# A batch's output products in one run over four PSUM banks, as 64-row and 64 by 64 tiles, and gamma's loads moved behind the first queries

## The chip, the cores and the metric

The kernel runs on one core of one Trainium2 chip. The metric is device microseconds of one execution. All ratios below are the mean time of one kernel's fast runs over the mean of the other's fast runs of the same rounds, so they are not quite the ratio of the medians that are quoted beside them. Under 1 is faster than the kernel before. The 95% interval is given in brackets.

The engines are TensorE (PE: matmuls; PEld: its weight loads), VectorE (DVE), ScalarE (ACT), GpSimd (POOL) and SyncE (SP, which issues most DMAs). L346 is a line of the kernel's source; the line numbers of the changed kernel differ from those of the kernel before.

## The reference, cut to what matters

A linear attention without softmax, a per-head norm, and then a gated feed-forward layer on all 4608 tokens:

```python
batch, n_heads, seq, head_dim = (8, 8, 576, 64)
kv  = np.einsum('bhsd,bhse->bhde', k, v)          # a 64 x 64 state per head
out = np.einsum('bhsd,bhde->bhse', q, kv)         # "output products"
out = out / sqrt(mean(out**2, axis=-1) + 1e-6) * g_norm
x   = out as [batch*seq, 512]
xn  = x / sqrt(mean(x**2, axis=-1) + 1e-6) * rms_g
y   = silu(xn @ w_gate) * (xn @ w_val) @ w_out    # d_ff = 1536
```

## The kernel before

Each batch has 576 tokens: 512 "main" tokens, and 64 "tail" tokens. The tails of all eight batches form a ninth block of 512. The feed-forward layer of block n runs in 16 units: units 0 to 11 are the up products (two groups of four 128x512 matmuls each, into `g_ps` and `v_ps`), units 12 to 15 the down products. Between those units the kernel places the attention of block n+1: state products, output products, squares, sums, norm.

The output products of a main block multiply transposed queries `qt` (two heads of 64 on 128 rows, 512 tokens) with a block-diagonal state `kv_all` (two 64x64 states on the diagonal of 128x128, zeros elsewhere). One group of 128 tokens took four 128x128 matmuls, at four different units:

```python
def o_products(self, c, ps):
    for j in range(NS):                      # NS = 4 pairs of heads
        cols = ps[:, 2 * j : 2 * j + 2, :]   # 128 columns of one PSUM bank
        if self.tail:
            for u in range(2):               # two batches' 64 tail tokens
                rows = slice(u * TAIL, (u + 1) * TAIL)
                PE.matmul(cols[rows], lhsT=tails_q["t"][:, c, j, rows],
                          rhs=kv_all[:, 2 * c + u, j, :], ...)
        else:
            PE.matmul(cols, lhsT=self.qt[:, j, 128 * c : 128 * c + 128],
                      rhs=kv_all[:, self.n, j, :], ...)
...
kv0, os = (3, (4, 5, 6, 7)) if n == 1 else (1, (2, 3, 5, 6))
steps[kv0] += [a.kv_products, a.kv_copy]     # a = attention of block n+1
for c, u in enumerate(os):
    cs = ((0, 1), (), (2, 3), ())[c] if a.tail else (c,)
    steps[u].append(lambda a=a, cs=cs: a.o_rows(cs))   # products
    steps[u].append(lambda a=a, c=c: a.put_o(c))       # squares and copy on ScalarE
    steps[u + 1].append(lambda a=a, c=c: a.sums(c))    # sums on VectorE
```

The opening handles batch 0 by hand. Its loads are issued in this order on the sync queue (the values of 0 and 1 on ScalarE's); index j is a pair of heads:

```python
for j in (0, 1):
    load_kv(0, "k", nc.sync, ...j);  load_kv(0, "v", nc.scalar, ...j)
load_q0(0, nc.sync)                                  # "the first queries"
for j in (2, 3):
    load_kv(0, "k", nc.sync, ...j);  load_kv(0, "v", nc.sync, ...j)
nc.sync.dma_start(out=gam[0:NS, :], in_=moe_rms_g...)     # gamma, 2 KB
nc.sync.dma_start(out=gam[NS:NS+1, :]..., in_=g_norm...)  # gamma, 0.5 KB
load_q0(1, nc.sync)
...                                                  # then the weights
```

For n = 1, ScalarE casts the values of batch 2 in units 0 and 1:

```python
steps[0] += [lambda i=i: cast_kv(2, "v", i, SC) for i in (0, 1)]
steps[1] += [lambda i=i: cast_kv(2, "v", i, SC) for i in (2, 3)]
```

## Time and profile before

| | before |
|---|---|
| median, range | 322.36 us (322.31 to 323.43, 3 runs) |
| span of the profiled run | 321.4 us |
| PE busy | 97% |
| granted PE clock | full on the page. But the page counts the stretch before the first clock record (5.2 us in this trace) as full, and there the 128x512 matmuls start 0.43 us apart, twice the later 0.216 us. In one trace the clock falls to half in the opening, from 13.0 to 16.4 us (see e4) |

The first lines are from the page of the kernel before: engine busy times, then rows of 40 slices of 8 us each, in tenths.

```profile
PE 311.0 (97%) x2011; PEld 154.1 (48%) x2047; DVE 179.6 (56%) x371; ACT 178.8 (56%) x319; POOL 20.3 (6%) x43
...
PE   7799999999999999999999999999999999999995
...
DMA  7999999987279747923893378948002600240014
...
PE 84%; DMA 10%; issue 1%; ACT 1%; another core or an unknown queue 1%; DVE 1%; SPq 0%; ACTq 0%
...
L346 PE MATMUL att_ps<-kv_all,qt 128*128 128x128 bf16 x96 | 9.3, 219 | 0.3
```

The reader sees two regimes: DMA is at 9 tenths or more in slices 2 to 8 (8 to 64 us), PE in all but the first two and the last. PE is the bound from about 62 us on (busy 63.62 of the 64 us from 62 to 126 us, 131.16 of the 132 us from 126 to 258 us). The L346 line lists the 96 main output products at 219 ns each, but within a group their records start 56 ns apart and overlap. What a run costs is therefore read from starts. These lines are the timeline of PE in the kernel before (start us, duration us, engine, line, operation, out<-in, count, and in brackets what idle time before it waited for), around one group of four output products, then around the two tail runs.

```profile
127.88 0.81 PE L479 MATMUL v_ps<-xnt,wv_sb 128*128 128x512 bf16 x3
128.53 0.39 PE L346 MATMUL att_ps<-kv_all,qt 128*128 128x128 bf16 x4
128.75 1.03 PE L479 MATMUL g_ps<-xnt,wg_sb 128*128 128x512 bf16 x4
...
258.35 0.81 PE L479 MATMUL v_ps<-xnt,wv_sb 128*128 128x512 bf16 x3
259.09 0.64 PE L341 MATMUL att_ps<-kv_all,qt 128*64 128x128 bf16 x16
259.66 0.60 PE L479 MATMUL g_ps<-xnt,wg_sb 128*128 128x512 bf16 x2
```

A 128x512 matmul starts every 0.216 us, so three from 127.88 us end their turn at 128.53 us. The four products then take until 128.75 us: 0.22 us, or 56 ns each. Four groups make 0.89 us a batch. In the tail, the turn ends at 259.00 us and the next 128x512 starts at 259.66 us: 0.66 us for 16 matmuls in 64-column tiles, 1.33 us for both tail runs. The first tail matmul comes 0.09 us late; here the tile in the records changes from `128*128` to `128*64`, and e6 below measures what a change of tiling costs.

The last two places are in the opening of the kernel before: the wait for gamma, and the wait at 61 us.

```profile
9.59 0.67 ACT L106 CAST vb<-st 128x576 bf16<-128x576 f32 x1 [0.97 <-DMA st<-in_v_dram]
10.32 0.47 PE L267 MATMUL att_ps<-vb,kb 64*64 64x64 bf16 x18 [0.55 <-ACT vb L106]
11.62 0.19 PE L715 MATMUL o_ps<-ident,gam 5*128 5x5 f32 x1 [0.84 <-DMA gam<-in_g_norm_dram]
12.39 0.47 PE L267 MATMUL att_ps<-vb,kb 64*64 64x64 bf16 x18
...
60.33 1.14 ACT L106 CAST vb<-st 128x512 bf16<-128x512 f32 x2 [2.15 <-DMA st<-in_v_dram]
62.01 0.38 PE L479 MATMUL g_ps<-xnt,wg_sb 128*128 128x512 bf16 x1 [0.26 <-ACT silu L484]
```

PE stands 0.84 us for gamma at 11.62 us. At 62.01 us it waits for a silu, which stood in ScalarE's queue behind casts that waited for the values of batch 2.

### The profile page before, as it was taken

The page shows a single profiled execution, that of the slowest core. Times are in us where ns is not written, and L with a number is a line of the kernel's source. Part 1 is how long each engine was busy: PE and PEld are TensorE (multiplying, and loading weights), DVE is VectorE, ACT ScalarE, POOL GpSimd, SP SyncE. Part 2 cuts the span into 40 slices and gives each one's busy share as a digit, 9 for nine tenths or more (in the row PEclk, how much of TensorE's full clock was granted, in tenths as well). Part 3 has the DMA queues.
Part 4 walks back from the last instruction along what each step waited for, and adds up shares of the span by engine and source line. Part 5 has one row for each costly group of instructions (what it writes and reads, how often), then busy time and mean ns, then how long its engine had stood idle before and what let it go on. Part 6 is the DMA issues. An engine that isn't in the chain of part 4 may idle for free.

```text
span 321.4 us, 5351 instructions
## 1 busy us (share of the span) xinstructions
PE 311.0 (97%) x2011; PEld 154.1 (48%) x2047; DVE 179.6 (56%) x371; ACT 178.8 (56%) x319; POOL 20.3 (6%) x43
## 2 busy tenths in 40 slices
PE   7799999999999999999999999999999999999995
PEld 3475456454445444544444444444544444444443
DVE  4685857569427932794279516951696058703310
ACT  3596457665767476647664766566554355233321
POOL 1253452100000000000000000000000000000000
PEclk9999999999999999999999999999999999999999
DMA  7999999987279747923893378948002600240014
GB/s 260 344 353 387 379 375 296 231 244 212 56 151 311 174 124 185 309 69 90 174 321 105 65 202 194 311 102 174 35 2 49 174 40 1 42 157 1 0 34 98
DMA packets 74439, 54.89 MB, mean 171 GB/s; under 512 B 42281, under 2 KB 67117, under 8 KB 74413
## 3 DMA queue, kind: packets, MB, share of 16 engines
q1 hardware_dynamic: 74044, 53.89, 59.9%
q10 hardware_dynamic: 368, 0.66, 0.6%
q8 instruction: 16, 0.26, 0.3%
q14 instruction: 11, 0.08, 0.1%
HBM read 37.75 MB, written 9.44 MB: 147 GB/s over the span
## 4 chain that ended last, share of the span: by engine, by line
PE 84%; DMA 10%; issue 1%; ACT 1%; another core or an unknown queue 1%; DVE 1%; SPq 0%; ACTq 0%
PE g_ps L479 27%; PE v_ps L479 26%; PE o_ps L521 24%; DMA st<-in_v_dram 3%; DMA st<-in_moe_w_out_dram 3%; PE att_ps L346 2%; DMA gam<-in_g_norm_dram 2%; DMA st<-in_k_dram 1%; PE att_ps L275 1%; DMA out_dram<-o_sb 1%; PE g_ps L496 1%; PE o_ps L496 1%; PE v_ps L496 1%; DVE xna L460 0%
## 5 line engine op out<-in xcount | busy, mean ns | idle before, releaser
L485 DVE TENSOR_TENSOR h_sb<-silu,v_ps 128x512 bf16<-128x512 bf16 x104 | 70.8, 683 | 107.8 <-ACT silu L484 68.7
L479 PE MATMUL g_ps<-xnt,wg_sb 128*128 128x512 bf16 x403 | 105.7, 379 | 1.3 <-ACT silu L484 0.3
L479 PE MATMUL v_ps<-xnt,wv_sb 128*128 128x512 bf16 x405 | 104.4, 379 | 0.1
L484 ACT ACTIVATE silu<-g_ps 128x512 bf16<-128x512 f32 x104 | 62.4, 601 | 61.9 <-PE g_ps L479 49.2
L521 PE MATMUL o_ps<-wo_sb,h_sb 128*128 128x512 bf16 x386 | 87.1, 379 | 0.5
L479 PEld LDWEIGHTS <-wv_sb 128*128 128x128 bf16 x416 | 40.7, 98 | 49.1 <-DVE wv_sb L204 0.2
L521 PEld LDWEIGHTS <-h_sb 128*128 128x128 bf16 x420 | 40.7, 98 | 47.9 <-issue 0.3
L479 PEld LDWEIGHTS <-wg_sb 128*128 128x128 bf16 x416 | 38.9, 98 | 42.3 <-issue 0.8
L106 ACT COPY o_sb<-o_ps 128x512 f32<-128x512 f32 (+1 forms) x34 | 19.7, 579 | 38.0 <-PE o_ps L521 35.3
L368 DVE TENSOR_REDUCE ssq<-sq 128x16 f32<-128x1024 bf16 x28 | 34.2, 1220 | 1.0
L359 ACT ACTIVATE sq<-att_ps 128x512 bf16<-128x512 f32 x28 | 16.7, 597 | 12.3 <-PE att_ps L346 7.9
L106 ACT CAST vb<-st 128x512 bf16<-128x512 f32 (+2 forms) x34 | 19.5, 626 | 5.7 <-DMA st<-in_v_dram 5.7
L385 DVE TENSOR_TENSOR xna<-outa,s1y 128x512 bf16<-128x512 bf16 x28 | 17.9, 684 | 0.0
L106 ACT CAST qb<-st 128x1024 bf16<-128x1024 f32 (+1 forms) x17 | 15.4, 943 | 2.3 <-DMA st<-in_q_dram 2.2
L361 ACT CAST outa<-att_ps 128x512 bf16<-128x512 f32 x28 | 16.3, 581 | 0.0
L106 ACT CAST kb<-st 128x512 bf16<-128x512 f32 (+1 forms) x25 | 14.0, 619 | 0.0
L367 DVE TENSOR_TENSOR sq<-sq,gsq 128x512 bf16<-128x512 bf16 x28 | 11.7, 418 | 0.0
L346 PEld LDWEIGHTS <-qt 128*128 128x128 bf16 x96 | 7.4, 98 | 5.7
L346 PE MATMUL att_ps<-kv_all,qt 128*128 128x128 bf16 x96 | 9.3, 219 | 0.3
L622 PE MATMUL att_ps<-kv_all 128*128 128x512 bf16 (+1 forms) x21 | 7.5, 486 | 1.2 <-DVE sel L611 1.2
L108 POOL CAST wo_sb<-st 128x512 bf16<-128x512 f32 x12 | 7.5, 654 | 7.0 <-DMA st<-in_moe_w_out_dram 7.0
L108 DVE CAST kb<-st 128x576 bf16<-128x576 f32 (+1 forms) x12 | 5.3, 459 | 2.5 <-DMA st<-in_k_dram 2.5
(139 smaller groups left out, 160.6 us busy)
## 6 DMA issues: line engine op xcount, KB each, us to landing
out_dram<-o_sb SPq DMA_DIRECT2D x14, 512.0 KB, 3.0
st<-in_q_dram SPq DMA_DIRECT2D x6, 1024.0 KB, 6.4
st<-in_k_dram SPq DMA_DIRECT2D x6, 1024.0 KB, 10.2
st<-in_v_dram SPq DMA_DIRECT2D x6, 1024.0 KB, 11.8
st<-in_moe_w_out_dram SPq DMA_DIRECT2D x6, 512.0 KB, 10.3
st<-in_moe_w_gate_dram SPq DMA_DIRECT2D x4, 512.0 KB, 8.4
st<-in_moe_w_val_dram SPq DMA_DIRECT2D x4, 512.0 KB, 9.1
st<-in_k_dram SPq DMA_DIRECT2D x4, 288.0 KB, 5.7
```

The lines of the kernel that those rows point to most:

```text
L106: engine.copy(out=dst, in_=src)
L108: engine.tensor_copy(out=dst, in_=src)
L346: PE.matmul(cols, lhsT=self.qt[:, j, 128 * c : 128 * c + 128], rhs=kv_all[:, self.n, j, :], start=(j == 0), stop=(j == NS - 1),)
L359: SC.activation(out=self.sq[c][:, 0], in_=ps, func=ACT.Square)
L361: SC.copy(out=self.outa[c], in_=ps)
L367: DVE.tensor_tensor(out=sq[:, 1], in0=sq[:, 0], in1=gsq8, op=OP.mult)
L368: DVE.reduce_sum(out=self.ssq[:, c], in_=sq, axis=AX.X)
L385: DVE.tensor_tensor(out=self.xna[c], in0=self.outa[c], in1=self.alpha[:, c, :].to_broadcast([128, H, D]), op=OP.mult)
L479: PE.matmul(ps, lhsT=wt[:, s, j * 128 : (j + 1) * 128], rhs=x[:, s, :], start=(s == 0), stop=(s == NS - 1),)
L484: SC.activation(out=silu, in_=g_ps, func=ACT.Silu)
L485: DVE.tensor_tensor(out=self.h[:, j, :], in0=silu, in1=v_ps, op=OP.mult)
L521: PE.matmul(self.o_ps[c], lhsT=self.h[:, j, c * 128 : (c + 1) * 128], rhs=wo_sb[:, j, :], start=(j == 0), stop=(j == NF - 1),)
```

## The change

The intent: use only the 64 rows and 64 columns that are not zero, let the two heads of a pair work in the two row halves of the array, do a whole block in one run (two banks of the attention pool and the two that the down products leave free), and fetch gamma before it is needed.

```diff
+        def o_products(self):
+            self.banks = [
+                [p.tile([128, 2, NS, D], FP32, name=nm) for _ in range(2)]
+                for p, nm in ((att_pool, "att_ps"), (ops_pool, "o_ps"))
+            ]
+            for c in range(T):
+                for j in range(NS):
+                    for g in range(2):                       # head parity = row half
+                        rows = slice(g * D, g * D + D)
+                        ps = self.banks[c // 2][g][:, c % 2, j, :]
+                        flags = ...
+                        if self.tail:
+                            for u in range(2):
+                                us = slice(u * TAIL, (u + 1) * TAIL)
+                                PE.matmul(ps[us], lhsT=tails_q["t"][rows, c, j, us],
+                                          rhs=kv_all[rows, 2 * c + u, j, rows], **flags)
+                        else:
+                            PE.matmul(ps, lhsT=self.qt[rows, j, 128 * c : 128 * c + 128],
+                                      rhs=kv_all[rows, self.n, j, rows], **flags)
...  # put_squares and put_rows read two banks each; pools regrouped in pairs
-            kv0, os = (3, (4, 5, 6, 7)) if n == 1 else (1, (2, 3, 5, 6))
+            kv0 = 1 + 2 * int(n == 1)
...
+            steps[kv0 + 1] += [a.o_products]
+            for i in range(2):
+                u = kv0 + 1 + 2 * i
+                steps[u] += [lambda a=a, i=i: a.put_squares(i)]
+                steps[u + 1] += [lambda a=a, i=i: a.put_rows(i)]
+                for c in range(2):
+                    steps[u + i + c] += [lambda a=a, c=2 * i + c: a.sums(c)]
...  # opening: gamma's two loads before keys and values 2, 3
     load_q0(0, nc.sync)
+    nc.sync.dma_start(out=gam[0:NS, :], ...)
+    nc.sync.dma_start(out=gam[NS : NS + 1, :]..., ...)
     for j in (2, 3):
         load_kv(0, "k", nc.sync, slice(j, j + 1))
         load_kv(0, "v", nc.sync, slice(j, j + 1))
-    nc.sync.dma_start(out=gam[0:NS, :], ...)
-    nc.sync.dma_start(out=gam[NS : NS + 1, :]..., ...)
...  # opening: weight rounding around the norm of the second half of batch 0
-    round_w(1, "g", 0, SC)
-    round_w(1, "g", 3, SC)
-    round_w(1, "g", 1, GP)
+    for s in range(2):
+        round_w(1, "g", s, GP)
     Z.head()
     Z.root_by_table(lambda: round_w(1, "g", 2, DVE))
+    round_w(1, "g", 3, SC)
```

More of the change, by code (lines that the diff above doesn't have):

```diff
@@ L59 @@
     qt_pool = pool("qt", 2)
-    outa_pool = pool("outa", 4)
-    sq_pool = pool("sq", 2)
+    outa_pool = pool("outa", 2)
+    sq_pool = pool("sq", 1)
     sqt_pool = pool("sqt", 1)
@@ L300, in __init__ @@
             self.sq = {}
-            self.o_ps = {}
             self.qt = None
@@ L333, in q_turn @@
             cast(engine, self.qt[:, :, 256 * pair : 256 * pair + 256], ps.rearrange("p j i t -> p j (i t)"))
-        def o_products(self, c, ps):
-            for j in range(NS):
-                cols = ps[:, 2 * j : 2 * j + 2, :]
-                if self.tail:
-                    for u in range(2):
-                        rows = slice(u * TAIL, (u + 1) * TAIL)
-                        PE.matmul(
-                            cols[rows], lhsT=tails_q["t"][:, c, j, rows], rhs=kv_all[:, 2 * c + u, j, :],
-                            start=(j == 0), stop=(j == NS - 1),
-                        )
-                else:
-                    PE.matmul(
-                        cols, lhsT=self.qt[:, j, 128 * c : 128 * c + 128], rhs=kv_all[:, self.n, j, :],
-                        start=(j == 0), stop=(j == NS - 1),
-                    )
@@ L351, in o_rows @@
-        def o_rows(self, cs):
-            for c in cs:
-                self.o_ps[c] = att_pool.tile([128, H, D], FP32, name="att_ps")
-                self.o_products(c, self.o_ps[c])
-        def put_o(self, c):
-            ps = self.o_ps[c]
-            self.sq[c] = sq_pool.tile([128, 2, H, D], BF16, name="sq")
-            SC.activation(out=self.sq[c][:, 0], in_=ps, func=ACT.Square)
-            self.outa[c] = outa_pool.tile([128, H, D], BF16, name="outa")
-            SC.copy(out=self.outa[c], in_=ps)
+        def o_products(self):
[8 more added lines that the diff above has]
+                        ps = self.banks[c // 2][g][:, c % 2, j, :]
+                        flags = dict(start=(c % 2 == 0 and j == 0), stop=(c % 2 == 1 and j == NS - 1))
+                        if self.tail:
+                            for u in range(2):
+                                us = slice(u * TAIL, (u + 1) * TAIL)
+                                PE.matmul(
+                                    ps[us], lhsT=tails_q["t"][rows, c, j, us], rhs=kv_all[rows, 2 * c + u, j, rows],
+                                    **flags,
+                                )
+                        else:
+                            PE.matmul(
+                                ps, lhsT=self.qt[rows, j, 128 * c : 128 * c + 128], rhs=kv_all[rows, self.n, j, rows],
+                                **flags,
+                            )
@@ new lines, in put_squares, with put_rows @@
+        def put_squares(self, i):
+            p, nm = ((sq_pool, "sq"), (sqt_pool, "sqt"))[i]
+            self.sq[i] = p.tile([128, 2, 2, H, D], BF16, name=nm)
+            for g in range(2):
+                SC.activation(out=self.sq[i][:, :, 0, g:H:2, :], in_=self.banks[i][g], func=ACT.Square)
+        def put_rows(self, i):
+            rows = outa_pool.tile([128, 2, H, D], BF16, name="outa")
+            for g in range(2):
+                SC.copy(out=rows[:, :, g:H:2, :], in_=self.banks[i][g])
+            for c in range(2):
+                self.outa[2 * i + c] = rows[:, c]
@@ L365, in sums @@
                 self.ssq = stat_pool.tile([128, T, 2, H], FP32, name="ssq")
-            sq = self.sq[c]
+            sq = self.sq[c // 2][:, c % 2]
             DVE.tensor_tensor(out=sq[:, 1], in0=sq[:, 0], in1=gsq8, op=OP.mult)
@@ L440, in o @@
             self.o_products(c, ps)
-            self.outa[c] = outa_pool.tile([128, H, D], BF16, name="outa")
+            if c % 2 == 0:
+                self.rows = outa_pool.tile([128, 2, H, D], BF16, name="outa")
+            self.outa[c] = self.rows[:, c % 2]
             cast(engine, self.outa[c], ps)
@@ L593 @@
     load_q0(0, nc.sync)
-    for j in (2, 3):
-        load_kv(0, "k", nc.sync, slice(j, j + 1))
-        load_kv(0, "v", nc.sync, slice(j, j + 1))
     nc.sync.dma_start(out=gam[0:NS, :], in_=moe_rms_g.rearrange("(s p) -> s p", p=128))
@@ L601 @@
     )
+    for j in (2, 3):
+        load_kv(0, "k", nc.sync, slice(j, j + 1))
+        load_kv(0, "v", nc.sync, slice(j, j + 1))
     load_q0(1, nc.sync)
@@ L985 @@
             a = atts[n + 1]
-            kv0, os = (3, (4, 5, 6, 7)) if n == 1 else (1, (2, 3, 5, 6))
+            kv0 = 1 + 2 * int(n == 1)
             if not a.tail:
                 steps[kv0] += [a.kv_products, a.kv_copy]
-            for c, u in enumerate(os):
-                cs = ((0, 1), (), (2, 3), ())[c] if a.tail else (c,)
-                steps[u].append(lambda a=a, cs=cs: a.o_rows(cs))
-                steps[u].append(lambda a=a, c=c: a.put_o(c))
-                steps[u + 1].append(lambda a=a, c=c: a.sums(c))
+            steps[kv0 + 1] += [a.o_products]
[3 more added lines that the diff above has]
+                steps[u + 1] += [lambda a=a, i=i: a.put_rows(i)]
+                for c in range(2):
+                    steps[u + i + c] += [lambda a=a, c=2 * i + c: a.sums(c)]
             late = 2 * int(n == 1)
```

## The prediction

> **What bounds the kernel now.** The page gives TensorE (PE) 311.0 of 321.4 us busy (97%), clock full in every slice; the chain of waits that ended last is 84% PE and 10% DMA. There are two regimes. Until about 62 us the DMA engines are 99-100% busy in the slices; the chain runs through a weight DMA and then the values of batch 2, landing at 60.3 us, and near 61.4 us PE idles 0.3-0.4 us behind it (ScalarE is held by casts of those values). From 62 to 314 us the timeline shows PE matmuls without a gap, one 128x512 every 216 ns. There only TensorE time counts: time saved on VectorE or ScalarE is worth nothing, unless it starts a stall.
>
> **What changes, costed.**
>
> 1. Output products of six batches (after 62 us). Before: four runs of four 128x128 matmuls, 55.7 ns from start to start, 16 x 55.7 = 0.89 us per batch, no change of tiling. After: one run of 32 matmuls with 64 rows, 64 columns moving, even and odd heads in alternating row halves. If two halves overlap, a pair should cost what pairs of 64-wide column tiles cost in the state products: 31.6 ns a pair (start to start, 40 matmuls in 0.63 us). [...] this trace shows it only for column tiles and 64x64 tiles, whose pairs start 2-4 ns apart. So 16 x 31.6 = 0.51 us. The run now changes tiling twice; [...] around the state products the matmul before and the one after lose 0.09 and 0.10 us. Total 0.71 us: estimated saving 0.18 us a batch, 1.1 us for six. If the 128-column weight loads of the two halves serialize (25 ns a load was the shortest spacing, in the sums), a pair costs 50 ns, a run 1.0 us, and the change loses 0.6 us.
>
> 2. Tail batch. Before: two runs of 16 column-tile matmuls, each 0.66 us from the end of the up product to the next one, 1.33 us. After: 64 matmuls of 64x64 in one run: 0.71 us if four overlap, 1.2 us if two do. Saving 0.1-0.6 us.
>
> 3. Gamma earlier. PE waited 0.84 us at 11.6 us for it (landed 11.48). Behind the first queries it should land near 8 us. Keys and values 2 and 3 are issued 1.4 us later, but the DMA queue has work until they start. The opening runs up to 0.8 us sooner, as may the moved weight rounding (0.3 us). But the DMA limit at 61 us does not move, so I expect nearly all of this to come back as a longer PE wait there: 0-0.3 us net.
>
> 4. Losses: all four transposed query blocks are now needed at the start of the run. For batch 2 the last landed at 66.7 us, for batch 3 at 96.4 us, just about when they will be read: 0-0.4 us of stall together. ScalarE and VectorE work keeps its size and fits.
>
> **Sum:** 322.36 - 1.1 - 0.35 - 0.15 + 0.3 = about 321.1 us; range 319.9 to 322.6. Faster over 2%: 0.01; within 2%: 0.97; slower: 0.02.
>
> **What would show it.** A run of a main batch 0.7 us between neighbouring 128x512 matmuls, pairs 2-4 ns apart at 32 ns; tail 0.7-1.2 us. The opening 0.5-0.8 us earlier at 20 us, but level with before at 63 us, with a wait on the batch-2 values grown by as much. PE still without gaps after 97 us.
>
> **What would make it wrong.** Row halves that do not overlap; the DMA stream finishing sooner because the opening does; late query transposes or the four held banks stalling PE.

## The result

The changed kernel took 321.67 us median (320.77 to 322.44, 6 runs) against 322.48 us (322.31 to 323.43, 6 runs): ratio 0.997 [0.9948, 0.9991]. It lies in the predicted range, 0.6 us above the predicted number. The profiled run's span is 320.4 us.

First the page of the changed kernel, then its PE timeline at the places shown of before.

```profile
PE 309.1 (96%) x2138; PEld 151.1 (47%) x2175; DVE 181.5 (57%) x371; ACT 178.9 (56%) x318; POOL 21.0 (7%) x44
...
PE 78%; DMA 14%; DVE 2%; SPq 2%; issue 1%; another core or an unknown queue 1%; ACT 1%; POOL 0%; ACTq 0%; DVEq 0%
```

```profile
128.29 0.81 PE L490 MATMUL v_ps<-xnt,wv_sb 128*128 128x512 bf16 x3
129.04 0.41 PE L354 MATMUL att_ps<-kv_all,qt 64*128 64x64 bf16 x16
129.28 0.40 PE L354 MATMUL o_ps<-kv_all,qt 64*128 64x64 bf16 x16
129.61 0.60 PE L490 MATMUL g_ps<-xnt,wg_sb 128*128 128x512 bf16 x2
...
257.90 0.81 PE L490 MATMUL v_ps<-xnt,wv_sb 128*128 128x512 bf16 x3
258.64 0.45 PE L349 MATMUL att_ps<-kv_all,qt 64*64 64x64 bf16 x32
258.92 0.46 PE L349 MATMUL o_ps<-kv_all,qt 64*64 64x64 bf16 x32
259.31 0.39 PE L490 MATMUL g_ps<-xnt,wg_sb 128*128 128x512 bf16 x1
```

The main run: the turn of the three 128x512 ends at 128.94 us, the next starts at 129.61 us, so 0.67 us where four groups cost 0.89 us. The records in between start in pairs, 3 to 4 ns apart, a pair every 29.2 ns. The tail run costs 259.31 - 258.55 = 0.76 us where two cost 1.33 us; its matmuls start in fours, one four every 31.6 ns.

The opening of the changed kernel:

```profile
10.31 0.67 ACT L106 CAST vb<-st 128x576 bf16<-128x576 f32 x1 [1.89 <-DMA st<-in_v_dram]
11.03 0.47 PE L267 MATMUL att_ps<-vb,kb 64*64 64x64 bf16 x18 [1.47 <-ACT vb L106]
11.43 0.22 PE L726 MATMUL o_ps<-ident,gam 5*128 5x5 f32 x1
12.31 0.47 PE L267 MATMUL att_ps<-vb,kb 64*64 64x64 bf16 x18
...
60.82 1.14 ACT L106 CAST vb<-st 128x512 bf16<-128x512 f32 x2 [2.56 <-DMA st<-in_v_dram]
62.50 0.38 PE L490 MATMUL g_ps<-xnt,wg_sb 128*128 128x512 bf16 x1 [0.67 <-ACT silu L495]
...
90.29 1.02 PE L490 MATMUL g_ps<-xnt,wg_sb 128*128 128x512 bf16 x4 [0.19 <-DMA xnt<-xna]
```

PE no longer waits for gamma, but the values of pair 2 are cast at 10.31 us instead of 9.59 us. The next state (the second L267) starts at 12.31 us instead of 12.39 us: of the 0.84 us, 0.08 us remains. At 61 us the values of batch 2 came 0.49 us later in this run, and at 90 us there is a new short wait for transposed rows. (In e4, a second trace of this kernel, neither wait is there.)

**How to separate the two regimes.** From the state products of block 4 (the third group of 40 matmuls of L275; the first is that of block 2) the traces repeat within 0.2 us, whatever happened before: 193.89 to 194.07 us in the seven traces that hold the changed kernel's product runs, beside 195.32 to 195.45 us in the three with those of the kernel before (table below). This line is from the PE timeline of the kernel before:

```profile
126.04 0.82 PE L275 MATMUL att_ps<-vb,kb 128*64 128x64 bf16 x40
```

and this from that of the changed kernel:

```profile
126.45 0.82 PE L275 MATMUL att_ps<-vb,kb 128*64 128x64 bf16 x40
```

The span less this start is the late part: 321.4 - 126.04 = 195.36 us before, 320.4 - 126.45 = 193.95 us after, 1.41 us less. It holds four main runs and the tail: 4 x 0.22 + (1.33 - 0.76) = 1.45 us. So the late part is understood. The early part holds two more main runs, which should have brought it forward by 0.45 us, but in this run it is 0.41 us longer. The experiments are about both parts.

### The profile page after: what moved, and what is told of

The parts are those of the page before. It is cut to its first block, busy times and chain, and to the rows that moved or that the text cites. A ratio compares the mean times of both kernels' runs of the same rounds, so it can differ in the third digit from the quotient of the medians.

```text
span 320.4 us, 5591 instructions
## 1 busy us (share of the span) xinstructions
PE 309.1 (96%) x2138; PEld 151.1 (47%) x2175; DVE 181.5 (57%) x371; ACT 178.9 (56%) x318; POOL 21.0 (7%) x44
## 4 chain that ended last, share of the span: by engine, by line
PE 78%; DMA 14%; DVE 2%; SPq 2%; issue 1%; another core or an unknown queue 1%; ACT 1%; POOL 0%; ACTq 0%; DVEq 0%
PE g_ps L490 26%; PE v_ps L490 25%; PE o_ps L532 22%; DMA st<-in_moe_w_out_dram 7%; DMA st<-in_moe_w_val_dram 3%; DMA st<-in_v_dram 2%; PE att_ps L275 1%; DMA st<-in_k_dram 1%; SPq L194 1%; DMA xnt<-xna 1%; DVE xna L394 1%; DMA out_dram<-o_sb 1%; PE att_ps L354 1%; SPq L401 1%
## 5 line engine op out<-in xcount | busy, mean ns | idle before, releaser
L490 PE MATMUL v_ps<-xnt,wv_sb 128*128 128x512 bf16 x409 | 106.1, 379 | 0.6
L490 PE MATMUL g_ps<-xnt,wg_sb 128*128 128x512 bf16 x398 | 104.6, 379 | 1.6 <-ACT silu L495 0.7
L377 DVE TENSOR_REDUCE ssq<-sqt 128x16 f32<-128x1024 bf16 x14 | 17.1, 1220 | 0.5
L377 DVE TENSOR_REDUCE ssq<-sq 128x16 f32<-128x1024 bf16 x14 | 17.1, 1220 | 0.5
L363 ACT ACTIVATE sq<-att_ps 128x512 bf16<-128x512 f32 x14 | 7.6, 594 | 4.3 <-PE att_ps L354 3.6
L376 DVE TENSOR_TENSOR sq<-sq,gsq 128x512 bf16<-128x512 bf16 x14 | 5.9, 422 | 4.9 <-ACT sq L363 4.9
L363 ACT ACTIVATE sqt<-o_ps 128x512 bf16<-128x512 f32 x14 | 7.6, 597 | 0.0
L368 ACT CAST outa<-att_ps 128x512 bf16<-128x512 f32 x14 | 7.5, 592 | 0.0
L368 ACT CAST outa<-o_ps 128x512 bf16<-128x512 f32 x14 | 7.5, 592 | 0.0
```

What stands on the lines that cost most here:

```text
L363: SC.activation(out=self.sq[i][:, :, 0, g:H:2, :], in_=self.banks[i][g], func=ACT.Square)
L368: SC.copy(out=rows[:, :, g:H:2, :], in_=self.banks[i][g])
L376: DVE.tensor_tensor(out=sq[:, 1], in0=sq[:, 0], in1=gsq8, op=OP.mult)
L377: DVE.reduce_sum(out=self.ssq[:, c], in_=sq, axis=AX.X)
L490: PE.matmul(ps, lhsT=wt[:, s, j * 128 : (j + 1) * 128], rhs=x[:, s, :], start=(s == 0), stop=(s == NS - 1),)
```

## The experiments

Twelve experiments ran, in four jobs; each job timed the kernel before again, so that row gives the span of those medians, the changed kernel's own job included. "Late part" is the span less the start of block 4's state products, both from the profiled run; "run" is the cost of one undisturbed main run, read as above.

The times and the spans do not differ by a constant. In the lists of runs, time less span is in the mean 1.79 to 1.81 us where GpSimd has 43 instructions (before, e1, e2), 1.91 to 1.95 us with 44 (the changed kernel, e3 to e6, e9), 2.03 to 2.09 us with 45 or 46 (e7, e8, e11, e12) and 2.33 us with 48 (e10). No run shows why, and the number of instructions may not be the cause. But the versions that give GpSimd more to do lost 0.1 to 0.5 us there, which no span and no late part shows.

| label | what it is | median us | ratio to before | run us | tail us | block 4 starts | late part us |
|---|---|---|---|---|---|---|---|
| before | | 322.5 to 323.1 | 1 | 4 x 0.22 | 2 x 0.66 | 126.04 | 195.36 |
| after | | 321.67 | 0.997 [0.9948, 0.9991] | 0.67 | 0.76 | 126.45 | 193.95 |
| e1_products | products alone | 321.38 | 0.9961 [0.9943, 0.998] | 0.67 | 0.76 | 125.26 | 193.94 |
| e2_gamma | gamma move alone | 322.98 | 1.0005 [0.9986, 1.0025] | 4 x 0.22 | 2 x 0.66 | 126.18 | 195.32 |
| e3_full_rows | one run, full tiles | 323.02 | 1.001 [0.9992, 1.0029] | 0.89 | 1.11 | 125.60 | 195.10 |
| e4_after_again | the changed kernel | 321.54 | 0.9955 [0.9932, 0.9978] | 0.67 | 0.76 | 126.31 | 193.89 |
| e5_halves_apart | other order | 321.73 | 0.9955 [0.9925, 0.9985] | 0.68 | 0.85 | 125.80 | 194.10 |
| e6_two_runs | two runs a block | 322.26 | 0.9979 [0.9951, 1.0006] | 2 x 0.44 | 2 x 0.47 | 124.97 | 194.93 |
| e7_gamma_pool | gamma on POOL's queue | 320.65 | 0.9928 [0.9906, 0.9949] | 0.67 | 0.76 | 124.72 | 193.98 |
| e8_casts_spread | casts moved | 321.36 | 0.995 [0.9925, 0.9976] | 0.67 | 0.76 | 125.41 | 193.89 |
| e9_one_half | one row half only (wrong result) | 324.28 | 1.0039 [1.0015, 1.0063] | 1.13 | 1.22 | 126.11 | 196.29 |
| e10_best | e7, e8 and a later batch 2 | 321.54 | 0.9949 [0.9929, 0.9969] | 0.67 | 0.76 | 124.69 | 194.01 |
| e11_before_gamma_pool | before, gamma on POOL | 322.52 | 0.9991 [0.9965, 1.0017] | 4 x 0.22 | 2 x 0.66 | 124.95 | 195.45 |
| e12_gamma_pool_again | e7 again | 320.83 | 0.9946 [0.9929, 0.9963] | 0.67 | 0.76 | 124.23 | 194.07 |

The theory (A): the gain is all in the products, because matmuls of the two row halves overlap; the gamma move gives nothing, because it displaces keys and values. Rivals: the gamma move is what gains (B); doing a block in one run is what gains (C); half as many columns is what gains, overlap or not.

### e1_products: the products alone

```diff
+    # before the weights: keys and values 2 and 3 first, gamma after them, as in the kernel before
+    # round_w(1, "g", ...) as in the kernel before
```

(Taken from the changed kernel, with the two opening edits undone.)

> The output products alone (four-bank run, row halves, 64x64 tail tiles), with gamma and the weight rounding as in the kernel before. Theory A (all gain comes from the products, and the gamma move costs about what it gives, or delays the batch-2 values): runs of 0.67 us and 0.76 us as in the changed kernel; the opening is that of before (state 2 starts at 10.3 us, PE waits for gamma at 11.6 us, restart near 62.0 us); span 1.0 to 1.9 us below before, ratio 0.994 to 0.997, at or below the changed kernel's. Rival B (the gamma move is worth its 0.8 us): this kernel is 0.5 to 0.8 us slower than the changed one, ratio 0.999 to 1.000.

Measured: 0.9961 [0.9943, 0.998]; the late part is the changed kernel's to 0.01 us. PE waited 0.85 us for gamma again (11.24 us, L726), and the kernel was still no slower than the changed one in its two jobs (0.997 and 0.9955). Rival B falls. The main runs of batches 2 and 3 cost 0.76 and 0.81 us here, 0.23 us in sum above the usual 0.67: their third or fourth query block had not arrived, a loss that the prediction listed.

### e2_gamma: the gamma move alone

```diff
     load_q0(0, nc.sync)
+    nc.sync.dma_start(out=gam...)   # both gamma loads
     for j in (2, 3): ...            # keys and values 2 and 3
-    nc.sync.dma_start(out=gam...)
```

> Gamma's two loads moved behind the first queries, nothing else changed from before. Theory A: keys and values 2 and 3 land 0.7 us later than before (values 2 at 10.3 instead of 9.6 us), so the opening gains under 0.1 us at 12 us, and nothing is left at 62 us: ratio 0.999 to 1.002. Rival B: the opening is 0.5 us or more earlier and the span 0.3 to 0.8 us shorter, ratio 0.997 to 0.999.

Measured: 1.0005 [0.9986, 1.0025], so the move alone is worth nothing that can be seen. Values 2 came late here too: they were cast at 10.08 us instead of 9.59 us, and PE stood 0.86 us for them. The views by windows show what the queue did. From 7 to 10 us it moved 341 GB/s here and 320 to 351 GB/s in the seven other traces with gamma behind the first queries; it moved 377 and 379 GB/s in the kernel before and e1, and 366 to 389 GB/s in the four traces with gamma on GpSimd's queue (below). Its engines were busy (0.93 to 1.01 of the time, against 1.01 to 1.05), but they moved less.

### e3_full_rows: one run, but full tiles

```diff
-    for g in range(2): PE.matmul(64 rows, 64 columns -> bank of the parity)
+    PE.matmul(self.banks[c][:, 2*j : 2*j+2, :], lhsT=self.qt[:, j, 128*c : 128*c+128],
+              rhs=kv_all[:, self.n, j, :], ...)   # the kernel before's matmul, into 4 banks
```

> The changed kernel, but the single run over four banks made of full 128x128 matmuls (and the tail of 64-wide column tiles with 128 moving columns). Theory A (the gain is the overlap of row halves on half as many columns): main run 0.89 us with no tiling change, tail run about 1.1 to 1.2 us (one entry and exit of the tiling instead of two); span 0.1 to 0.3 us at most below before, ratio 0.998 to 1.002. Rival C (the gain comes from doing a batch in one run, not from the tiles): a main run well under 0.89 us and a span like the changed kernel's, ratio 0.995 to 0.997.

Measured: 1.001 [0.9992, 1.0029]. The PE timeline of this kernel:

```profile
127.22 1.03 PE L483 MATMUL v_ps<-xnt,wv_sb 128*128 128x512 bf16 x4
128.09 0.61 PE L347 MATMUL att_ps<-kv_all,qt 128*128 128x128 bf16 x8
128.53 0.61 PE L347 MATMUL o_ps<-kv_all,qt 128*128 128x128 bf16 x8
128.98 1.03 PE L483 MATMUL g_ps<-xnt,wg_sb 128*128 128x512 bf16 x4
```

The run lasts from 128.09 to 128.98 us, 0.89 us: what the four groups cost. Rival C falls for main blocks. For the tail, the one run does save one entry and exit: 1.11 us against 1.33 us, and the late part shrinks by 0.26 us.

### e4_after_again: a second trace of the changed kernel

> The changed kernel once more, for a second trace. If the two losses seen in its first trace (restart after the batch-2 values at 62.5 instead of 62.0 us, and a wait of 0.35 us for the transposed rows at 90 us) come from the change, both appear again; if they are scatter of the DMA stream, one or both vanish and the span falls by as much, to 319.5 or 319.9 us. Ratio 0.995 to 0.998.

Measured: 0.9955 [0.9932, 0.9978]. Both losses of the first trace were scatter: here nothing waits at 61 us, and the wait for transposed rows at 90 us is gone. But block 4 starts just as late, at 126.31 us, and this trace shows something else. These lines are the view by windows of this run (window, its length, busy times and counts of PE, PEld, DVE, ACT and POOL, then the granted PE clock, DMA share and GB/s):

```profile
10.00:12.00 2.00, 0.78 (x21) 0.70 (x21) 1.54 (x4) 1.16 (x2) 0.00 (x0) 1.00 1.05 350
12.00:14.00 2.00, 2.00 (x25) 0.90 (x24) 1.34 (x8) 1.02 (x3) 0.42 (x1) 0.75 1.05 360
14.00:16.00 2.00, 2.00 (x21) 1.44 (x20) 1.02 (x5) 0.95 (x3) 1.05 (x3) 0.50 1.10 354
16.00:18.00 2.00, 1.76 (x18) 1.30 (x17) 1.29 (x2) 1.14 (x3) 1.89 (x5) 0.90 1.09 345
```

The clock is at half from 13.0 to 16.4 us, after PE had stood 1.7 us for values 2:

```profile
11.22 0.47 PE L267 MATMUL att_ps<-vb,kb 64*64 64x64 bf16 x18 [1.69 <-ACT vb L106]
```

What lowered the clock is not shown. The length of the wait is not a sure cause: the changed kernel's first trace waited 1.47 us at the same place and has no dip (its clock is recorded as full from 4.7 to 318.7 us).

What the dip cost this run can be read off. The stretch from the first to the second pair of matmuls with `epsrow` (14.03 to 19.06 us, L432) takes 5.03 us here and 4.29 to 4.32 us in all other traces: 0.7 us more. The lists of runs give only a mean clock: 3.4 us at half clock is 0.005 of the span, so 0.995 or less is taken as the mark of such a dip, an estimate from this trace (the 0.997 of the first trace comes from the clock falling at 318.7 us, behind the last matmul). In the twelve runs of the changed kernel's two jobs, the four with such a clock have spans of 319.8 to 320.5 us (mean 320.2), the eight others 318.3 to 320.4 us (mean 319.4). The runs with the mark are thus some 0.8 us longer in the mean; with four runs against eight, and the two groups overlapping, that is no more than agreement with the 0.7 us. Runs of the kernel before have the mark as well (2 of the 11 beside this one, at 321.6 and 321.7 us).

### e5_halves_apart: four of one half, then four of the other

```diff
-            for c in range(T):
-                for j in range(NS):
-                    for g in range(2):
+            order = [(c, j, g) for c in range(T) for g in range(2) for j in range(NS)]
+            for c, j, g in order:
```

> The changed kernel with the two row halves of a 128-token block one after the other (four matmuls of one half, then four of the other) instead of alternating; the tail's order changes in the same way. Theory A (the gain is that alternating halves overlap): within a half the matmuls cannot overlap, so a run costs about 32 x 29 ns + 0.2 = 1.1 us instead of 0.67, 0.45 us more in each of six batches, 2.5 to 3 us in all: about 324.3 us, ratio to before 1.003 to 1.007. Rival (64 moving columns are cheap whatever the order): runs stay near 0.67 us and the span near the changed kernel's.

Measured: 0.9955 [0.9925, 0.9985], a run 0.68 us. The expectation failed. The 32 starts are 15.0 ns apart on average, half of what matmuls of one half take (29.5 ns in e9 below), so they still overlap. And the second matmul to start in the trace carries the wait on VectorE's semaphore, which in the program is the condition of the fifth, the first of the other half (a build of this kernel has it there). In this trace, then, a matmul of one half started ahead of three earlier ones of the other half. So this edit did not take the overlap away, and could not test it.

### e9_one_half: the overlap itself

```diff
-                        rows = slice(g * D, g * D + D)
+                        rows = slice(0, D)        # both parities: wrong results on purpose
```

> Wrong results on purpose: in the changed kernel both members of a pair read rows 0 to 63, so no two of the run's matmuls use different row halves; number and sizes stay. The run before this one with halves four matmuls apart did not slow down, because the trace shows matmuls of the other half starting ahead of their turn. Theory A (different halves overlap, and that is the whole gain): here they cannot, a main run costs about 32 x 29 ns + 0.2 = 1.1 us instead of 0.67, the tail more than 1.0 instead of 0.76: 2.5 to 3 us slower than the changed kernel, ratio to before 1.003 to 1.007. Rival (half the moving columns is the gain): runs stay near 0.67 us.

Measured: 1.0039 [1.0015, 1.0063], with a wrong result, as meant. The PE timeline of this kernel:

```profile
127.73 1.03 PE L490 MATMUL v_ps<-xnt,wv_sb 128*128 128x512 bf16 x4
128.69 0.64 PE L354 MATMUL att_ps<-kv_all,qt 64*128 64x64 bf16 x16
129.17 0.63 PE L354 MATMUL o_ps<-kv_all,qt 64*128 64x64 bf16 x16
129.73 1.04 PE L490 MATMUL g_ps<-xnt,wg_sb 128*128 128x512 bf16 x4
```

Same counts, same sizes, but the run costs 129.73 - 128.60 = 1.13 us, with matmuls 29.5 ns apart. Theory A holds, and half as many columns without overlap are no gain: without overlap the 64-row tiles would be slower than the full ones (1.13 against 0.89 us), and with it they are faster (0.67 us). The late part is 196.29 us, 2.34 us above the changed kernel's; 4 x (1.13 - 0.67) + (1.22 - 0.76) = 2.30 us.

### e6_two_runs: what a change of tiling costs

```diff
-            steps[kv0 + 1] += [a.o_products]
             for i in range(2):
                 u = kv0 + 1 + 2 * i
+                steps[u] += [lambda a=a, i=i: a.o_products(i)]   # blocks 2i and 2i+1
```

> The changed kernel with each batch's products in two runs of two blocks, two units apart, instead of one of four. If entering and leaving the tiling costs 0.2 us each time, a run costs 0.43 us, two of them 0.87 against 0.67: 0.2 us more in each of seven batches, less 0.1 to 0.2 us in all for query blocks that are no longer waited for in batches 2 and 3: 1.1 to 1.3 us slower than the changed kernel, ratio to before 0.998 to 1.001. If the change of tiling were free, the two kernels would be level.

Measured: 0.9979 [0.9951, 1.0006]. The PE timeline of this kernel, around the first of two runs:

```profile
126.60 1.03 PE L490 MATMUL v_ps<-xnt,wv_sb 128*128 128x512 bf16 x4
127.56 0.41 PE L354 MATMUL att_ps<-kv_all,qt 64*128 64x64 bf16 x16
127.90 1.04 PE L490 MATMUL g_ps<-xnt,wg_sb 128*128 128x512 bf16 x4
```

Two runs of 0.44 us replace one of 0.67 us, so the extra entry and exit costs 0.20 us a main block; the tail pays 2 x 0.47 - 0.76 = 0.18 us. The late part is 0.98 us longer than the changed kernel's: 4 x 0.20 + 0.18. So the one run over four banks is not the gain (e3), but it is what keeps the gain: in four runs the entries and exits, an estimate by the same count, would cost 3 x 0.20 = 0.6 us a block more, and one run saves 0.22 us.

### e7_gamma_pool and e12_gamma_pool_again: gamma early, without displacing anything

```diff
+    nc.gpsimd.dma_start(out=gam[0:NS, :], in_=moe_rms_g...)      # before all other loads
+    nc.gpsimd.dma_start(out=gam[NS:NS+1, :]..., in_=g_norm...)
     ...
-    nc.sync.dma_start(out=gam...)                                # both, on the sync queue
```

(On the changed kernel.)

> The changed kernel with gamma's two loads issued from the otherwise idle GpSimd queue at the start, so that keys and values 2 and 3 keep their early place. Theory A (the move failed because it displaced keys and values 2 and 3, and the DMA stream ends the opening anyway): values 2 land near 9.6 us, PE does not wait for gamma, the opening is 0.7 us earlier than before at 12 us; at 61 us the wait for the values of batch 2 takes most of this back: span 0 to 0.4 us below the changed kernel, ratio 0.994 to 0.997. If instead the start sets the end of the opening, the span falls by 0.7 us or more below the changed kernel, ratio 0.993 or less.

Measured: 320.65 us, 0.9928 [0.9906, 0.9949]. These lines are from its timeline:

```profile
9.87 0.67 ACT L106 CAST vb<-st 128x576 bf16<-128x576 f32 x1 [1.47 <-DMA st<-in_v_dram]
10.59 0.47 PE L267 MATMUL att_ps<-vb,kb 64*64 64x64 bf16 x18 [1.05 <-ACT vb L106]
```

Values 2 are cast at 9.87 us (10.31 us in the changed kernel; 9.46 us in e12). PE does not wait for gamma, but still 1.05 us for them. The next state starts at 11.88 us, 0.43 us sooner than in the changed kernel. All six runs have a clock of 0.998 or more. Block 4 starts at 124.72 us, the late part is the changed kernel's. The ratio lies where the expectation put the case that the start does set the end of the opening: this trace has no wait at 61 us that takes the gain back.

> The changed kernel with gamma on the GpSimd queue once more, because the ratio of its first job (0.9928) leaned on a before with one run of 324.9 us, and the kernel before with the same move gained only 0.1%. If the version truly beats the changed kernel (0.997 and 0.9955 in its two jobs), the ratio is 0.992 to 0.995 again and most runs show a clock of 0.998 or more; if the first job was luck, it is 0.995 to 0.997.

Measured: 320.83 us, 0.9946 [0.9929, 0.9963] (one execution of the kernel before in that job took 664 us and is no fast run). Both jobs give the same picture: the medians are some 0.8 us below those of the changed kernel, but the intervals of e12 and e4 overlap, so the lead over the changed kernel is likely and not proven. Two things speak for it. In the four traces with gamma on GpSimd's queue (e7, e10, e11, e12) block 4 starts at 124.23 to 124.95 us, in the ten others at 124.97 to 126.45 us. And none of the 24 runs of these four kernels has a clock of 0.995 or less; 15 of the 91 other fast runs with a listed clock do.

### e11_before_gamma_pool: the same move on the kernel before

> The kernel before with gamma's two loads on the GpSimd queue and nothing else. If gamma really gates the opening and the opening counts: 0.5 to 1.0 us below before, ratio 0.997 to 0.9985, with the clock at 1.0 in most runs [...]. If the DMA limit near 61 us takes it all back: 0.9985 to 1.001.

The edit is that of e7 on the kernel before. Measured: 0.9991 [0.9965, 1.0017]: inconclusive, no gain that can be told from none. In its profiled run block 4 started at 124.95 us, 1.1 us sooner than in that of the kernel before, but its six times spread from 321.90 to 323.90 us. In spans it is 0.7 us below before in the mean (320.6 against 321.3 us); 0.2 us of that is lost outside the span.

### e8_casts_spread: the wait at 61 us

```diff
-            steps[0] += [lambda i=i: cast_kv(2, "v", i, SC) for i in (0, 1)]
-            steps[1] += [lambda i=i: cast_kv(2, "v", i, SC) for i in (2, 3)]
-            steps[0] += [lambda name=name: cast_kv(2, name, NS, GP) for name in ("k", "v")]
+            steps[0] += [lambda: cast_kv(2, "k", NS, GP)]
+            steps[0] += [lambda i=i: cast_kv(2, "v", i, GP) for i in (0, 1)]
+            steps[0] += [lambda: cast_kv(2, "v", NS, GP)]
+            steps[1] += [lambda: cast_kv(2, "v", 2, SC)]
+            steps[2] += [lambda: cast_kv(2, "v", 3, SC)]
```

> The changed kernel with the casts of the batch-2 values taken off ScalarE's way: two on GpSimd, one each a unit later on ScalarE. Theory A (near 61 us PE waits because ScalarE's silu is queued behind casts that wait for the values): the gap near 61 us is gone, the products of the states at n=1 begin 0.3 to 1.0 us sooner, span 0.3 to 0.8 us below the changed kernel, ratio 0.992 to 0.995. If PE waits there for the values themselves, the wait moves to the state products and the span stays.

Measured: 0.995 [0.9925, 0.9976]: level with the changed kernel. There is no gap at 61 us in this trace, but that settles nothing: e1, e4, e5, e6, e7, e9, e11 and e12 kept the casts and have no gap there either. That ScalarE's queue holds PE when there is a gap is read from the traces of before and after (silu starts at 61.37 and 61.86 us, as the two casts end); it is not shown by this experiment. The expected 0.3 to 0.8 us did not come.

### e10_best: removing the waits one after the other

```diff
+    # e7's gamma loads and e8's casts
-            kv0 = 1 + 2 * int(n == 1)
+            kv0 = 1 + 3 * int(n == 1)
```

> The kernel with gamma on the GpSimd queue, with the batch-2 value casts spread as tried before and, for batch 2 alone, states and products one unit later, so that the products no longer wait for the transposed queries (0.33 us at 65 us in the trace of gamma on GpSimd). If those two waits are all that is left after the opening, the product run of batch 2 costs 0.67 us, no gap stands near 61 us, and the span is 0.2 to 0.6 us below gamma on GpSimd alone: ratio to before 0.991 to 0.993. If the end of the opening is set by DMA data elsewhere, it stays at 0.993.

Measured: 0.9949 [0.9929, 0.9969], no better than e7. The run of batch 2 cost 0.67 us and no gap stood at 61 us, as expected. But the PE timeline of this kernel shows the waits one batch later:

```profile
88.18 1.02 PE L490 MATMUL g_ps<-xnt,wg_sb 128*128 128x512 bf16 x4
...
94.56 0.28 PE L354 MATMUL o_ps<-kv_all,qt 64*128 64x64 bf16 x8
95.01 0.29 PE L354 MATMUL o_ps<-kv_all,qt 64*128 64x64 bf16 x8 [0.17 <-DMA qt<-qb]
```

The first of these matmuls starts 0.26 us late (0.474 us after the one before it, where starts are 0.216 us apart otherwise), and the run of batch 3 costs 1.01 us, 0.35 us of it waiting for transposed queries. Block 4 starts at 124.69 us, as in e7 at 124.72 us. In this trace, what the early part won was given back at the next transposed block, up to 95 us. It is no fixed limit: e12, the kernel of e7, ran batches 2 and 3 without these waits (0.67 us each) and started block 4 at 124.23 us. In time less span, e10 also lost the most (2.33 us).

## Why the prediction was right or wrong, point by point

**What bounds the kernel: right in kind, the border was set too early.** From block 4 on, only PE time counts, to 0.1 us. But PE still waited for DMAs past 62 us, where the prediction drew the line: e1 waited for query blocks in batches 2 and 3 (0.23 us), and e10 shows waits up to 95 us (0.35 us of them in the run of batch 3).

**Step 1, main products: right, a little small.** Pairs at 29.2 ns instead of 31.6 ns, a run 0.67 us instead of 0.71 us, 0.22 us saved a batch instead of 0.18 us. That the halves overlap was the author's estimate, from the pairs of column tiles and of 64x64 tiles in the trace of the kernel before (2 to 5 ns from start to start). In the trace of the changed kernel the two of a pair start 3 to 4 ns apart, and e9 shows that without the overlap there is no gain (1.13 us a run). Entry and exit of the tiling were put at 0.19 us from the state products (0.09 and 0.10 us lost before and after them); e6 measured 0.20 us.

**Step 2, tail: right, at the upper end.** Four tiles overlap: 0.76 us, a saving of 0.57 us where 0.1 to 0.6 us was given and 0.35 us was counted.

**Step 3, gamma: the net result near zero was right, the reason was partly wrong.** "The DMA queue has work until they start" was the failing step. The queue stayed busy, but from 7 to 10 us it moved 320 instead of 377 GB/s, and keys and values 2 and 3 landed later: values 2 were cast at 10.31 instead of 9.59 us, and PE stood for them instead of for gamma. Why fewer bytes were moved stays open. The opening did not run 0.5 to 0.8 us sooner; at 12 us it was 0.08 us ahead (0.30 us in e2). The moved rounding was not tested alone; its 0.3 us cannot be seen, as the stretch that holds it (from the second `epsrow` pair to the first whole 128x512 up product) took 8.17 to 8.63 us in the four traces with the old order and 8.17 to 8.74 us in the others. So there was little gain to lose at 61 us; the later landing of values 2 had taken it at 10 us. e7 and e12, where gamma goes through another queue, are likely better by several tenths, which is what the move was meant to bring.

**Step 4, losses: right in size for the changed kernel.** 0.23 us for query blocks in e1, 0.09 us in e4 (runs of 0.70 and 0.73 us), none in the profiled run of the changed kernel. Other traces lost more: 0.33 us in e7 (batch 2), and 0.56 us in e5 (runs of 1.12 and 0.81 us).

**The sum: inside the range, but from two errors.** The products save 6 x 0.22 + 0.57 = 1.9 us of PE time, more than the 1.45 us counted. The measured 0.3% and 0.45% are 1.0 and 1.5 us. The late part returned 1.41 us; 0.14 us were lost outside the span (1.94 instead of 1.80 us). In both traces of the changed kernel the 0.45 us of batches 2 and 3 did not come back (in e1's trace, with block 4 at 125.26 us, they did); that the DMA stream sets the early part is the likely reading, not shown. How much of the missing rest is the clock's dip, and how much the changed order of loads, stays open: single traces of the early part scatter from 124.2 to 126.5 us. That the two errors, products counted too small and the early part too well, nearly cancelled is luck.

## What to carry to other kernels

In these runs small matmuls with 64 rows paid only when both row halves worked at the same time (a run of 0.67 us, against 1.13 us in one half and 0.89 us with full tiles). A pair then took the time of one of them (29.2 ns, against 29.5 ns for one in e9), and entering and leaving the tiling once more cost 0.2 us (e6); do enough of them in one run to cover that. In this kernel, whose DMA engines are busy at 9 tenths or more from 8 to 64 us, moving gamma's 2.5 KB forward moved larger loads back (values 2 were cast at 10.31 instead of 9.59 us); look at what the next load in line feeds before you gain a wait and lose another. To judge tenths of a per cent, find a point in the trace after which the runs repeat, and compare the part behind it; here the part behind repeated within 0.2 us, while the point itself came at 124.2 to 126.5 us.
